# Moving the early key and value sums of an attention and feed-forward kernel from VectorE and ScalarE to GpSimd, with a new order of instructions

## The chip, the cores and the metric

The kernel runs on one core of a Trainium2 chip. The metric is the time of one execution on the device in microseconds (us), as the median of several runs. Engines are named as in the profile: PE is TensorE, PEld its weight loads, DVE is VectorE, ACT is ScalarE, POOL is GpSimd, SP is the engine whose queue issues most of the transfers (SPq). All five work through their own queue strictly in order, and wait for each other by semaphores.

## What is computed

The reference is an attention with pooled keys and values, and a gated feed-forward layer on its result:

```python
k_p = k.reshape(B, H, Sp, pool, D).mean(axis=3)      # B=8, H=8, S=576, D=64, pool=8: 72 keys
v_p = v.reshape(B, H, Sp, pool, D).mean(axis=3)
scores = scale * np.matmul(q, k_p.transpose(0, 1, 3, 2))
scores = scores - np.max(scores, axis=-1, keepdims=True)
attn = np.exp(scores)
attn = attn / (np.sum(attn, axis=-1, keepdims=True) + 1e-09)
return np.matmul(attn, v_p)
...
x = attn_out.transpose(0, 2, 1, 3).reshape(B * S, H * D)      # 4608 x 512
gate = 1.0 / (1.0 + np.exp(-(x @ w_gate)))                    # w_gate, w_val 512 x 1536, w_out 1536 x 512
val = x @ w_val
return (gate * val @ w_out)
```

The mean over 8 neighbours of the sequence is made as a sum of 8; the factor 1/8 goes into the scale of the keys and into the denominators of the softmax. Weights arrive as 8-byte floats and are converted on the chip (w, raw), then split into a high and a low part (parts, oparts), so that three fast matmuls stand for one exact one.

## The kernel before, in words

The 4608 rows are cut into nine blocks of 512 rows, numbered j from 0. Heads go in pairs p (four pairs, 128 partitions). A block of 512 rows does not end where a batch of 576 ends, so block 1 needs the keys and values of batches 0 and 1, block 2 those of batches 1 and 2.

The function `first_pass` computes the attention of blocks 0, 1 and 2 and the feed-forward layer of block 0, while the weights arrive. Afterwards the blocks go two by two through a form that saves matmuls (`hidden`, `second_sums`), while the attention of later blocks (`attention`) is fitted in between. The change touches `first_pass` alone.

For the steps of this text, these names matter. In `first_pass`, `keys(j, p)` sums eight neighbours of the raw keys (a DVE reduction of 128x576 to 128x72 into the array that the profile calls early; raw, raws and h are the rooms of raw inputs). `place_keys` writes the two halves, scaled, into one of five buffers kbd, by two ACT instructions. `scores` multiplies queries with kbd on PE (tile sc); `maximum` and `exps` follow on DVE and ACT (tile e or early). `v_sum` and `r_sum` sum the raw values: the first 64 pooled values of each head on 128 partitions (128x512 to 128x64), the last eight on 96 partitions. `v_hi` casts a value sum (vh, ACT), `v_lo` subtracts (vl, DVE), `r_hi`, `r_lo` and `v_put` do the same for the last eight (other, vres), and `product_av` multiplies on PE. For block 0 the value sums are made by PE (vp, vr), for blocks 1 and 2 by DVE. `conv` steps turn raw weights into parts (four steps alternate between ACT and DVE), `product_of` makes the products with the gate and value weights (tile chain), `gate` and `h_of` apply the sigmoid (y) and multiply, `accumulate` multiplies with the third weight (tile acc).

The helper `pool(out, raw, eng)` is a single reduction on VectorE, and for another engine three additions of halves, in place in the raw tile:

```python
n = POOL // 2
while n > 1:
    eng.tensor_tensor(out=raw[:, :, :n], in0=raw[:, :, :n], in1=raw[:, :, n:2 * n], op=ALU.add)
    n //= 2
eng.tensor_tensor(out=out[:, :, None], in0=raw[:, :, :1], in1=raw[:, :, 1:2], op=ALU.add)
```

Every instruction of the whole program is first recorded by a small layer (`Book`, `Taken`), as units, and then issued in the order of the table LATER, a list of unit numbers. This table alone sets where an instruction stands in the queue of its engine; waits follow from the data. A second table, UNREAD, says how many matmuls with an unread result PE does ahead of some products (in the profile: sc, chain, av or tr, from cst or from kbd alone). Since all instructions go through the recording layer, the profile gives them one line (L319), and they are told apart by their tiles.

Of the kernel before, what the change touches and what calls it, by code (L numbers as in the profile page):

```python
# [61 lines left out]
    "sc.0.1.1": 10, "sc.0.1.0": 1, "sc.0.0.1": 1, "sc.0.2.0": 5, "sc.0.3.1": 7, "sc.0.3.0": 2, "sc.1.0.0": 1,  # L62
    "rturn.0.1": 5, "av.0.3": 1, "mm.0.0": 1, "mm.0.1": 5, "mm.1.0": 2, "mm.1.1": 1, "mm.0.2": 1, "sc.1.1.0": 1,
# [268 lines left out]
def attention_then_ffn(ctx: ExitStack, tc: tile.TileContext, qT, kT, vm, vr, vn, sums8, wgv, wo, const, out, outT):  # L332
# [759 lines left out]
    def first_pass():  # L1092
# [79 lines left out]
        def keys(j, p):  # L1172
            k = raws["k", j, p] if j else got[f"k{p}"].rearrange("p (g t) -> p g t", t=POOL)
            nc.vector.reduce_sum(out=ks[j, p][:, :KEYS], in_=k, axis=AX.X)
# [87 lines left out]
        def v_sum(j, p):  # L1262
            pool(vs[j, p], raws["v", j, p], nc.vector)
# [199 lines left out]
```

## Time and profile before

| what | value |
|---|---|
| median of 3 runs | 934.22 us (932.6 to 936.99) |
| the profiled execution, its own time | 933.27 us |
| its span, first to last instruction | 931.5 us |
| granted clock of TensorE over the span | 0.999 |
| busy: PE, DVE, ACT, POOL | 918.0, 695.0, 572.4, 24.1 us |
| instructions: PE, DVE, ACT, POOL | 4375, 1062, 1044, 59 |

The profiled execution takes 1.8 us beside its span, and lies 0.95 us below the median. Rows of a group read: engine, operation, output tile and inputs, shapes, count, then busy time in us and the mean of one in ns, then idle time of the engine in front of them and what ended it. A window row gives the busy time of each engine in a stretch of the span, with the number of instructions in brackets, then the granted clock, the mean share of the DMA engines and their rate. A busy PE is not PE at its peak, since matmuls overlap and their ends are modelled.

### The profile page before, as it was taken

Reading aid. Unit: us, or ns where it says so; the run is one execution under the profiler, and the core shown is the slowest. Engines: PE = TensorE matmul, PEld = TensorE weight load, DVE = VectorE, ACT = ScalarE, POOL = GpSimd, SP = SyncE. Lnnn points to the kernel's source line nnn. Section 1 sums busy time; section 2 is a strip of 40 time slices with the busy share of each in tenths; the row PEclk is TensorE's granted clock in tenths of the full one; section 3 lists DMA queues with packets and bytes.
Section 4 is the critical chain, followed back from the end, with each engine's and each line's share of the span. In section 5 each row is a group of like instructions: output and inputs, shape, how many; then the busy total and the mean of one; then the engine's idle time right before and its main releaser. Section 6 shows DMA issues by size and latency. Waiting matters only on the chain.

```text
span 931.5 us, 12557 instructions
## 1 busy us (share of the span) xinstructions
PE 918.0 (99%) x4375; PEld 756.0 (81%) x4375; DVE 695.0 (75%) x1062; ACT 572.4 (61%) x1044; POOL 24.1 (3%) x59
## 2 busy tenths in 40 slices
PE   8999999999999999999999999999999999999998
PEld 7778788887888878888888888888888878888886
DVE  6998888899999997976789956464768573544763
ACT  7999998679989764665575636443554353234442
POOL 1000000011121000000000000000000000000000
PEclk9999999999999999999999999999999999999999
DMA  9999496778889757787667567545456675566266
GB/s 341 372 354 346 164 392 226 254 264 304 289 303 340 265 192 262 265 301 243 210 212 235 191 223 232 191 166 186 156 193 203 216 235 191 177 198 191 94 212 192
DMA packets 90367, 223.13 MB, mean 240 GB/s; under 512 B 9536, under 2 KB 28480, under 8 KB 88768
## 3 DMA queue, kind: packets, MB, share of 16 engines
q1 hardware_dynamic: 85184, 203.97, 64.9%
q0 software_dynamic: 5120, 18.35, 5.1%
q8 instruction: 35, 0.57, 0.2%
q14 instruction: 28, 0.23, 0.1%
HBM read 168.81 MB, written 53.48 MB: 239 GB/s over the span
## 4 chain that ended last, share of the span: by engine, by line
PE 92%; ACT 5%; DMA 2%; DVE 1%; issue 0%; POOL 0%; ACTq 0%; POOLq 0%
PE chain L319 54%; PE acc L319 27%; PE sc L319 4%; PE av L319 4%; PE tp L319 2%; ACT e L319 1%; DMA parts<-keptV0C 1%; DMA oparts<-keptS 1%; ACT w L319 1%; ACT L319 1%; DMA oparts<-keptO 0%; ACT raw L319 0%; ACT y L319 0%; PE vp L319 0%; ACT parts L319 0%
## 5 line engine op out<-in xcount | busy, mean ns | idle before, releaser
L319 PE MATMUL chain<-xo,parts 128*128 128x512 f32 x2316 | 558.6, 394 | 2.9 <-ACT y L319 1.4
L319 PEld LDWEIGHTS chain<-xo,parts 128*128 128x128 f32 x2316 | 427.2, 188 | 93.4 <-ACT y L319 2.1
L319 PE MATMUL acc<-hs,oparts 128*128 128x512 f32 (+1 forms) x1011 | 235.3, 390 | 0.8 <-DMA oparts<-keptO 0.5
L319 PEld LDWEIGHTS acc<-hs,oparts 128*128 128x128 f32 x1011 | 188.2, 188 | 41.6 <-issue 1.4
L319 DVE TENSOR_TENSOR hs<-h,hs 128x1024 fp32r<-128x1024 f32 x52 | 63.3, 1221 | 37.9 <-ACT hs L319 37.5
L319 ACT CAST hs<-h 128x1024 fp32r<-128x1024 f32 x52 | 54.6, 1053 | 52.6 <-PE acc L319 51.4
L319 DVE TENSOR_TENSOR y<-chain,sG 128x512 f32<-128x512 f32 x69 | 47.2, 686 | 45.6 <-PE chain L319 32.3
L319 DVE TENSOR_TENSOR y<-chain,sV 128x512 f32<-128x512 f32 x69 | 47.2, 686 | 37.3 <-PE chain L319 25.8
L319 ACT COPY sV<-chain 128x512 f32<-128x512 f32 x69 | 40.3, 586 | 52.4 <-PE chain L319 48.6
L319 ACT COPY sG<-chain 128x512 f32<-128x512 f32 x69 | 40.4, 586 | 48.3 <-PE chain L319 47.7
L319 ACT ACTIVATE gate<-y 128x512 f32<-128x512 f32 x69 | 43.2, 631 | 39.7 <-DVE y L319 35.2
L319 ACT CAST hs<-s 128x1024 fp32r<-128x1024 f32 x36 | 37.9, 1054 | 39.8 <-PE acc L319 24.2
L319 ACT ACT_TABLE_LOAD x47 | 60.3, 1283 | 1.4 <-DVE y L319 0.5
L319 DVE TENSOR_TENSOR hs<-s,hs 128x1024 fp32r<-128x1024 f32 x36 | 44.0, 1221 | 14.6 <-ACT hs L319 14.4
L319 DVE TENSOR_TENSOR h<-y,gate 128x512 f32<-128x512 f32 x69 | 47.4, 689 | 3.8 <-ACT gate L319 1.8
L319 PE MATMUL sc<-kbd,raw 128*128 128x144 f32 (+1 forms) x260 | 41.0, 295 | 1.0 <-ACT other L319 0.7
L319 PEld LDWEIGHTS sc<-kbd,raw 128*128 128x128 f32 (+1 forms) x260 | 33.5, 177 | 9.8 <-issue 2.8
L319 PE MATMUL acc<-oparts,hs 128*128 128x512 f32 x144 | 37.8, 399 | 0.1
L319 DVE TENSOR_REDUCE m<-sc 128x4 f32<-128x288 f32 x48 | 21.7, 452 | 14.3 <-PE sc L319 14.0
L319 PEld LDWEIGHTS acc<-oparts,hs 128*128 128x128 f32 x144 | 26.3, 188 | 5.5 <-ACT pr L319 0.3
L319 DVE TENSOR_TENSOR h<-h 128x256 f32<-128x256 f32 (+2 forms) x39 | 28.3, 728 | 0.7
L319 ACT ACTIVATE gate<-chain 128x512 f32<-128x512 f32 x23 | 13.8, 599 | 18.9 <-PE chain L319 18.5
(193 smaller groups left out, 1026.0 us busy)
## 6 DMA issues: line engine op xcount, KB each, us to landing
oparts<-keptS SPq DMA_DIRECT2D x48, 512.0 KB, 4.1
oparts<-keptO SPq DMA_DIRECT2D x72, 256.0 KB, 3.5
raw<-in_wgv SPq DMA_DIRECT2D x12, 1024.0 KB, 8.7
out<-o SPq DMA_DIRECT2D x35, 256.0 KB, 4.4
raw<-in_kT SPq DMA_DIRECT2D x28, 288.0 KB, 4.8
raw<-in_qT SPq DMA_DIRECT2D x29, 256.0 KB, 4.4
raw_o<-in_wo SPq DMA_DIRECT2D x12, 512.0 KB, 6.7
keptO<-oparts SPq DMA_DIRECT2D x12, 512.0 KB, 3.8
```

Of the source, the lines that this page charges most:

```text
L319: return self._book.take(lambda: f(*args, **named))
```

## The change

For blocks 1 and 2 the sums of keys (8), of values (8) and of the last values (4) go from one VectorE reduction each to three GpSimd additions each, and the 16 ScalarE instructions that place scaled keys become 16 GpSimd instructions. Block 0 stays as it was. The list of steps of the first pass (ORDER) is the same; the table UNREAD holds other numbers, and the table LATER is another one.

```diff
 UNREAD = {
-    "sc.0.1.1": 10, "sc.0.1.0": 1, "sc.0.0.1": 1, "sc.0.2.0": 5, "sc.0.3.1": 7, "sc.0.3.0": 2, "sc.1.0.0": 1,
-    "rturn.0.1": 5, "av.0.3": 1, "mm.0.0": 1, "mm.0.1": 5, "mm.1.0": 2, "mm.1.1": 1, "mm.0.2": 1, "sc.1.1.0": 1,
+    "sc.0.1.1": 9, "sc.0.1.0": 1, "sc.0.0.1": 4, "sc.0.0.0": 6, "sc.0.2.1": 3, "sc.0.2.0": 3, "sc.0.3.1": 4,
+    "rturn.0.0": 1, "turn.0.1": 2, "sc.0.3.0": 5, "sc.1.0.1": 3, "av.0.0": 1, "rturn.0.1": 2, "turn.0.3": 1,
+    "av.0.3": 1, "mm.0.0": 3, "mm.0.1": 1, "mm.1.1": 1,
 }
...
 LATER = """
-2 17 15 11 34 5 10 35 19 14 6 36 12 8 3 37 18 4 7 38 16 9 39 13 28 40 41 20 42 43 24 46 58 90 25 91 92 23 26 93 94 79
...
         def keys(j, p):
             k = raws["k", j, p] if j else got[f"k{p}"].rearrange("p (g t) -> p g t", t=POOL)
-            nc.vector.reduce_sum(out=ks[j, p][:, :KEYS], in_=k, axis=AX.X)
+            pool(ks[j, p][:, :KEYS], k, nc.gpsimd if j else nc.vector)
...
             for r, c in ((slice(0, D), slice(0, KEYS)), (slice(D, P), slice(KEYS, 2 * KEYS))):
-                nc.scalar.activation(t[r, c], ks[j, p][r, :KEYS], AF.Copy, scale=SCALE)
+                if j:
+                    nc.gpsimd.tensor_scalar(out=t[r, c], in0=ks[j, p][r, :KEYS], scalar1=SCALE, scalar2=None, op0=ALU.mult)
+                else:
+                    nc.scalar.activation(t[r, c], ks[j, p][r, :KEYS], AF.Copy, scale=SCALE)
...
         def v_sum(j, p):
-            pool(vs[j, p], raws["v", j, p], nc.vector)
+            pool(vs[j, p], raws["v", j, p], nc.gpsimd if j else nc.vector)
...
         def r_sum(j, g):
-            pool(vsr[j, g][:96], raws["r", j, g], nc.vector)
+            pool(vsr[j, g][:96], raws["r", j, g], nc.gpsimd if j else nc.vector)
```

What the new table and the new engine make of the queues is seen in the order of the instructions. First GpSimd, at the start of the program, before: the last zeroing of buffers (vh, vl), and behind it the transfers of the next stage (keptG4A and the like).

```order
L319 MEMSET kbd_90 128x144
L319 MEMSET vh_93 128x128
L319 MEMSET vl_102 128x128
L319 MEMSET vh_95 128x128
L319 MEMSET vl_99 128x128
L319 DMA keptG4A<-parts 128x1024
L319 DMA keptG4B<-parts 128x1024
```

The same place with the change (raw is a raw tile of values or of keys, early the array of the sums, kbd_92 a buffer of placed keys):

```order
L322 MEMSET vl_100 128x128
L322 MEMSET vl_101 128x128
L322 MEMSET vl_102 128x128
L322 ISA
L322 TENSOR_TENSOR raw<-raw 128x64x4
L322 TENSOR_TENSOR raw<-raw 128x64x2
L322 TENSOR_TENSOR early<-raw 128x64
L322 TENSOR_TENSOR raw<-raw 128x72x4
L322 TENSOR_TENSOR raw<-raw 128x72x2
L322 TENSOR_TENSOR early<-raw 128x72
L322 TENSOR_SCALAR kbd_92<-early 64x72
```

A value sum, a key sum and its placing come in between, and a new instruction ISA ahead of the first addition, which the built program calls a reload of the library of GpSimd. The transfers of the next stage stand behind all 76 new arithmetic instructions.

Second VectorE, in the first pass, where weights are converted, before (w and raw_o are weights on the way, parts and oparts their split form, sc the scores):

```order
L319 TENSOR_REDUCE early<-raw 128x72
L319 TENSOR_TENSOR parts<-w_259,parts 128x2x256
L319 TENSOR_SCALAR w_265<-w_265 128x1024
L319 TENSOR_TENSOR parts<-w_245,parts 128x2x256 x2
L319 SCALAR_TENSOR_TENSOR w_265<-w_265,raw_225 128x1024
L319 TENSOR_SCALAR w_o<-w_o 128x1024
L319 TENSOR_REDUCE early<-raw 128x72
L319 SCALAR_TENSOR_TENSOR w_o<-w_o,raw_o 128x1024
L319 TENSOR_REDUCE early<-raws 96x64
L319 TENSOR_REDUCE early<-sc 128x4
L319 TENSOR_REDUCE early<-raw 128x72
```

The same place with the change:

```order
L322 TENSOR_REDUCE early<-sc 128x4
L322 TENSOR_SCALAR w_259<-w_259 128x1024
L322 TENSOR_TENSOR parts<-w_245,parts 128x2x256
L322 TENSOR_TENSOR vl_102<-early,vh_97 64x64
L322 TENSOR_TENSOR parts<-w_245,parts 128x2x256
L322 SCALAR_TENSOR_TENSOR w_259<-w_259,raw_226 128x1024
L322 TENSOR_SCALAR w_o<-w_o 128x1024
L322 SCALAR_TENSOR_TENSOR w_o<-w_o,raw_o 128x1024
L322 TENSOR_TENSOR parts<-w_259,parts 128x2x256
L322 TENSOR_TENSOR h<-chain,y 128x512
```

Four reductions of raw tiles are gone from eleven rows, what is left is conversion of weights, and the first product of the feed-forward layer (h) has moved up into it.

Third ScalarE at the start, with the change: the exponentials of block 0 (e, early), and among them the cast vh_97 of the value sum that GpSimd makes first.

```order
L322 ACTIVATE e<-sc,early 128x72 x8
L322 ACTIVATE kbd_91<-early 64x72 x2
L322 ACTIVATE early<-sc,early 128x72 x4
L322 CAST vh_97<-early 64x64
L322 ACTIVATE w_235<-raw_221 128x1024
L322 ACTIVATE early<-sc,early 128x72 x5
L322 ACTIVATE raw_221<-raw_221,cst 128x1024
```

And the same place before:

```order
L319 ACTIVATE e<-sc,early 128x72 x5
L319 ACTIVATE early<-sc,early 128x72 x4
L319 CAST vh_97<-early 64x64
L319 ACTIVATE kbd_91<-early 64x72
L319 ACTIVATE w_235<-raw_221 128x1024
L319 ACTIVATE early<-sc,early 128x72 x2
L319 ACTIVATE raw_221<-raw_221,cst 128x1024
```

The cast keeps its place, ahead of the first conversion of weights (w_235); what it waits for is now made by GpSimd in place of VectorE.

307 rows, old and new, of the table LATER are left out of this document.

## The prediction

> **What bounds the kernel now.** I read the page first: it says which engine the whole span hangs on.
>
> ```profile
> span 931.5 us, 12557 instructions
> PE 92%; ACT 5%; DMA 2%; DVE 1%; issue 0%; POOL 0%; ACTq 0%; POOLq 0%
> ```
>
> The second line is the chain of waits that ended last. PE holds 92% of it, ScalarE 5% (about 47 us), VectorE 1%. So the change, which adds no useful PE work and removes none, can only gain where PE stands behind ScalarE or VectorE. Busy time by stage shows where that is:
>
> ```profile
> core 0: us, PE busy (x) PEld busy (x) DVE busy (x) ACT busy (x) POOL busy (x), PEclk, DMA share, GB/s
> 0.00:20.00 20.00, 16.29 (x107) 15.01 (x108) 12.07 (x25) 13.25 (x45) 2.48 (x19) 1.00 0.94 328
> 20.00:60.00 40.00, 37.69 (x200) 29.51 (x199) 38.69 (x69) 37.76 (x80) 0.00 (x0) 1.00 1.01 385
> 60.00:100.00 40.00, 39.90 (x199) 32.56 (x198) 36.95 (x62) 37.80 (x82) 0.00 (x0) 1.00 0.85 297
> 100.00:160.00 60.00, 58.88 (x296) 48.01 (x295) 48.31 (x77) 56.26 (x107) 0.00 (x0) 1.00 0.71 272
> 160.00:400.00 240.00, 238.62 (x1151) 195.15 (x1150) 222.48 (x371) 179.76 (x354) 21.60 (x40) 1.00 0.80 275
> 400.00:931.50 531.50, 526.62 (x2433) 435.73 (x2431) 336.50 (x461) 247.60 (x384) 0.00 (x0) 1.00 0.62 201
> ```
>
> From 20 to 160 us ScalarE is busy 131.8 of 140 us. VectorE is as full to 60 us (38.69 of 40) and then loosens, to 48.31 of 60. PE is idle only 2.31 + 0.10 + 1.12 = 3.5 us there, and from 160 us on 6.3 us, most of it at the very end. The granted clock is 1.00 throughout, so no clock is to be won. GpSimd does nothing from 20 to 160 us. The chain of waits, asked for 20 to 160 us alone, says who holds it there:
>
> ```profile
> by line: PE chain L319 35.7%; PE acc L319 18.8%; PE av L319 7.7%; PE sc L319 5.0%; ACT w L319 3.8%; ACT L319 3.7%; ACT e L319 3.4%; ACT raw L319 2.8%; ACT y L319 2.4%; ACT hs L319 1.3%; issue 1.3%; ACT early L319 1.1%; ACT parts L319 1.1%;
> ```
>
> The ScalarE names add to 19.6% of 140 us, 27.4 us; no VectorE name is among the thirteen largest. So in this stage it is ScalarE that PE waits for now and then, and VectorE hardly ever.
>
> **What leaves ScalarE.** Sixteen placements of scaled keys go.
>
> ```profile
> L319 ACT ACTIVATE kbd<-early 64x72 f32<-64x72 f32 x24 | 6.3, 263 | 2.5 <-DVE early L319 2.3
> ```
>
> Sixteen of these 24 at 263 ns are 4.2 us, fourteen of them inside 20 to 160 us. Upper bound of the gain: ScalarE's queue is the bound all along, and the whole 4.2 us reaches PE. Lower bound: the gain counts only while ScalarE holds the chain, so fourteen times 0.263 us, 3.7 us, times 27.4 / 131.8, which is 0.8 us. I take 2.5 us, the middle, because between 20 and 60 us both queues are so full that ScalarE's lead would show, and after 60 us PE has little idle time left to give.
>
> **What leaves VectorE.** Twenty reductions, by these rows for 5 to 110 us:
>
> ```profile
> L319 DVE TENSOR_REDUCE early<-raw 128x72 f32<-128x576 f32 x8 | 5.9, 742 | 0.0
> L319 DVE TENSOR_REDUCE early<-raws 128x64 f32<-128x512 f32 x4 | 2.7, 678 | 0.0
> L319 DVE TENSOR_REDUCE early<-raws 96x64 f32<-96x512 f32 x4 | 2.6, 672 | 0.0
> L319 DVE TENSOR_REDUCE early<-raw 128x64 f32<-128x512 f32 x3 | 2.0, 675 | 0.0
> L319 DVE TENSOR_REDUCE early<-early 128x64 f32<-128x512 f32 x1 | 0.7, 667 | 0.0
> ```
>
> 5.9 + 2.7 + 2.6 + 2.0 + 0.7 = 13.9 us. I put this at nothing: with VectorE shorter, ScalarE, which was as full, is late next. If that cover fails the gain is larger (first rival).
>
> **What comes to GpSimd.** Sixty additions and sixteen placements. No row shows arithmetic there; the nearest are its zeroing of a kbd buffer and VectorE's own two-input work at the same sizes:
>
> ```profile
> L319 POOL MEMSET kbd<- 128x144 f32 x5 | 1.0, 221 | 0.3 <-POOLq L1454 0.3
> L319 DVE TENSOR_TENSOR parts<-h,parts 128x256 fp32r<-128x256 f32 x9 | 3.7, 420 | 0.0
> L319 DVE TENSOR_TENSOR r<-rest,r 128x128 fp32r<-128x128 f32 x18 | 5.1, 283 | 0.5 <-ACT r L319 0.5
> L319 DVE TENSOR_TENSOR vl<-vs,vh 64x64 fp32r<-64x64 f32 x40 | 8.7, 217 | 4.7 <-ACT vh L319 4.0
> ```
>
> At VectorE's pace a sum is 0.42 + 0.28 + 0.22 = 0.92 us, twenty are 18.4 us, and sixteen placements at 0.22 us are 3.5 us: 22 us at least. At three times that pace it would be 59 us, still inside the 100 us or so over which the inputs arrive and are used, so the engine itself is no bound. The Trainium skill (GPSIMD Engine Reference, section Performance versus the Vector engine) gives 4497 ns against VectorE's 2293 ns for an addition of 2048 elements; by that factor 1.96 the additions would be 36 us and the whole, as an estimate, 40 us.
>
> Where the new queue waits: each placement waits until PE has read the old keys, and the sums behind it stand still meanwhile. The placement of kbd_89, for one, waits for the first scores from a kbd and raws, with later sums behind it. In the chain of waits they are this piece:
>
> ```profile
> 43.62 0.84 PE sc L319 x6
> ```
>
> The sums behind belong to scores and products much later than that, so I put it at nothing. The weight transfers of the next stage stand behind all this on the same queue, but their first was issued after an idle time of 162.7 us:
>
> ```profile
> L319 POOL DMA_DIRECT2D keptG4A<-parts x1 | 0.7, 671 | 162.7 <-DVE parts L319 162.7
> ```
>
> So 22 to 59 us of new work ahead of them cost nothing.
>
> **What moves on SP and PE.** The first load of values goes from seventh to fourth place in SP's queue. At the 328 GB/s of the first window its 256 KB hold the loads behind it back by 0.8 us; between 0 and 0.8 us, I take 0.3 us, since only half of block 0's first loads stand behind it. The unread matmuls go from 44 to 51. What they cost is seen in the rows for 20 to 60 us:
>
> ```profile
> L319 PE MATMUL chain<-cst 128*128 128x128 f32 x20 | 3.3, 286 | 0.9 <-DVE xo L319 0.9
> L319 PE MATMUL tr<-cst 128*128 128x128 f32 x10 | 1.3, 282 | 0.0
> L319 PE MATMUL sc<-cst 128*128 128x128 f32 x4 | 0.8, 273 | 0.0
> L319 PE MATMUL av<-cst 128*128 128x128 f32 x2 | 0.4, 275 | 0.0
> ```
>
> Each counts as two instructions, 0.33 us by the first row, so seven more are 2.3 us at most. They stand where PE waits anyway, so I take nothing, and nothing up to 2.3 us for the range. The new table moves everything else as well, up to the last stage; the 6.3 us of PE idle time after 160 us is what it could win, and by the same measure lose. I take 0, and 2 us to either side.
>
> **The sum.** 933.27 - 2.5 + 0.3 = 931.1 us for the profiled execution; it lay 0.95 us below the median of the runs, so the median to expect is 932.0 us. Its own range is 928 to 938.5 us: 934.2 - 4.2 - 2 one way; 934.2 - 0.8 + 0.8 + 2.3 + 2 the other.
>
> **Rival one: VectorE's relief counts too.** From 20 to 60 us it is the fuller of the two (38.69 us), and nine of the twenty reductions start between these two, its timeline says:
>
> ```profile
> 37.74 0.74 DVE L319 TENSOR_REDUCE early<-raw 128x72 f32<-128x576 f32 x1
> ...
> 58.48 0.75 DVE L319 TENSOR_REDUCE early<-raw 128x72 f32<-128x576 f32 x1
> ```
>
> Then the two queues shrink together, and what PE gives up is its waiting: the 3.5 us of idle time and the 3.3 + 1.3 + 0.8 + 0.4 = 5.8 us of unread matmuls of 20 to 60 us, 9.3 us at most. With 8 us of it gone the median is 926.2 us. For it speaks the order, in which the first h stands among the conversions and not after them; against it that the chain has no VectorE name of weight, and that UNREAD has grown.
>
> **Rival two: GpSimd's additions hold VectorE up.** Work on tiles in memory that VectorE does with two inputs, or at twice its pace, is the bulk of its load from 5 to 110 us:
>
> ```profile
> L319 DVE TENSOR_TENSOR parts<-w,parts 128x512 fp32r<-128x512 f32 x18 | 12.2, 684 | 1.7 <-ACT parts L319 1.6
> L319 DVE SCALAR_TENSOR_TENSOR w<-w,raw 128x1024 uint32<-128x1024 uint32 x9 | 11.0, 1219 | 0.7 <-ACT raw L319 0.6
> L319 DVE TENSOR_SCALAR w<-w 128x1024 f32<-128x1024 f32 x9 | 6.2, 684 | 0.6 <-ACT w L319 0.6
> ```
>
> If every GpSimd instruction kept such work waiting for its whole time, VectorE would get back 22 us for the 13.9 us it loses, 8 us net, of which the 1.31 + 3.05 = 4.4 us that it is idle from 20 to 100 us swallow half. The 3.7 us left are more than ScalarE's 2.5 us; add 0.3 us of SP, and the median is 935.7 us; with half as many meetings VectorE breaks even and the forecast stands. Before, the two engines never worked side by side in this stage, so no row speaks for or against it. The Trainium skill (SBUF — State Buffer, section Who interferes with whom) says just this: a VectorE instruction with two inputs in SBUF, and a GpSimd instruction that reads SBUF, exclude each other, the second waits for the first to end. By that rule alone, with the 40 us estimated above all spent in VectorE's way, 40 - 13.9 - 4.4, 21.7 us, would come on top of the forecast: 954 us, as an estimate; I don't expect so many meetings, since reductions and work on PSUM are free of it.
>
> **Rival three, slower: the first sum comes too late.** ScalarE's cast of a value sum stands in front of its first conversion of weights, and nothing passes it. These rows are from the timelines of POOL, DVE, ACT and PE:
>
> ```profile
> 2.81 0.20 POOL L319 MEMSET vl<- 128x128 f32 x1
> 11.43 0.68 DVE L319 TENSOR_REDUCE early<-raw 128x64 f32<-128x512 f32 x1
> 14.13 0.26 ACT L319 CAST vh<-early 64x64 fp32r<-64x64 f32 x1
> 17.01 0.74 DVE L319 TENSOR_REDUCE early<-raw 128x72 f32<-128x576 f32 x1
> 21.75 0.91 PE L319 MATMUL sc<-kbd,raw 128*64 128x144 f32 x6
> ```
>
> GpSimd is free at 3.0 us and ScalarE asks at 14.1 us; PE's first scores of block 1 ask for the first placed keys at 21.75 us. In between stand the new ISA instruction, a reload of code that no row prices, and 0.92 us of additions, twice that before the keys. Each microsecond that the first sum ends after 14.1 us is lost on ScalarE, and through it on PE. The rival decides from 14.1 + 4.7 + 2.2 = 21 us on, when reload and sum take 18 us; at 24 us the loss is 9.9 us, against 2.2 us gained, and the median is 941.9 us. The Trainium skill (GPSIMD Engine Reference, section Instruction dispatch) puts the load of code ahead of a first call at about 6 us; by that, as an estimate, the sum is there at about 10 us and this rival falls.
>
> **How the numbers follow.** About 0.5%, 4.7 us, is what a measurement of this kernel can tell from no change. Forecast (932.0 us) 0.42; rival one (926.2 us) 0.25; rival two (935.7 us) 0.14; rival three (941.9 us and more) 0.19. Faster than 929.5 us are rival one and the lower end of the forecast, together 0.31. Slower than 938.9 us are rival three but for its mild end, 0.17, and the bad end of rival two, 0.06: 0.23. The rest, 0.46, is no change that can be told. The range 924 to 942 us leaves out the far half of rival three and a little of rival one.
>
> **What would show it.** Right: kbd and the sums leave ACT and DVE, GpSimd is busy 22 to 60 us more, ScalarE's share of the chain from 20 to 160 us is a little smaller, and PE reaches the same matmuls of the next stage 2 to 3 us earlier. Rival one: PE's idle time and unread matmuls in 20 to 60 us shrink by more than 5 us. Rival two: the mean of parts, 684 ns, or of w, 1219 ns, grows in the first 100 us. Rival three: a wait of ScalarE's vh or PE's sc for POOL before 30 us. The prediction is wrong at its root if the difference arises after 160 us, from the table alone.

## The result, and the profile after

With the change the kernel takes 929.18 us (median of eight runs, 928.23 to 932.44), and 934.72 us without it in the same series: a ratio of 0.9947, 95% interval 0.9931 to 0.9963. By this ratio it is 5 us less, within 3.5 and 6.4 (the two medians lie 5.5 us apart). The forecast was 932.0 us, 2.2 us less; the measured time lies inside its range of 924 to 942 us, on the edge between "no change" and "faster". The profiled execution took 929.36 us. Its page, span and busy times:

```profile
span 927.5 us, 12645 instructions
PE 916.7 (99%) x4389; PEld 758.9 (82%) x4389; DVE 690.1 (74%) x1042; ACT 568.0 (61%) x1028; POOL 76.2 (8%) x135
PE 83%; ACT 5%; DVE 4%; DMA 3%; issue 3%; POOL 1%; SPq 0%; POOLq 0%; ACTq 0%; DVEq 0%
```

GpSimd has 52.1 us more (76.2 against 24.1), within the 22 to 59 us foreseen. ScalarE has 4.4 us less, as it should. VectorE has lost 13.9 us of reductions but is only 4.9 us shorter: something gave most of it back. (Not all 9 us of that is owed to GpSimd's reading: in the run e7 below, where GpSimd only fills, VectorE is 10.5 us shorter than before, at 684.5 us, so the reading takes 5.6 us.) Its rows up to 112 us, to be laid beside the 684 and 1219 ns of before, with three of the additions and the placements behind them:

```profile
L322 DVE TENSOR_TENSOR parts<-w,parts 128x512 fp32r<-128x512 f32 x18 | 15.0, 846 | 0.6 <-ACT parts L322 0.5
L322 DVE SCALAR_TENSOR_TENSOR w<-w,raw 128x1024 uint32<-128x1024 uint32 x9 | 12.3, 1369 | 0.4
L322 DVE TENSOR_TENSOR oparts<-w_o,oparts 128x1024 fp32r<-128x1024 f32 x3 | 4.6, 1523 | 0.0
L322 POOL TENSOR_SCALAR kbd<-early 64x72 f32<-64x72 f32 x16 | 10.3, 641 | 26.9 <-PE sc L322 26.0
L322 POOL TENSOR_TENSOR raw<-raw 128x288 f32<-128x288 f32 x8 | 6.9, 860 | 11.4 <-DMA raw<-in_kT 11.4
L322 POOL TENSOR_TENSOR raw<-raw 128x144 f32<-128x144 f32 x8 | 5.6, 701 | 0.5
L322 POOL TENSOR_TENSOR early<-raw 128x72 f32<-128x72 f32 x8 | 3.4, 421 | 0.6
```

The work of VectorE with two inputs in memory has grown: 18 × 0.162 + 9 × 0.150 + 3 × 0.31, with oparts at 1213 ns before, is 5.2 us in these three rows. That is the mechanism of rival two, here with the forecast's outcome. Rival three stayed away: GpSimd waited for its data, and before 30 us nobody waited for a sum or for placed keys. GpSimd's timeline, and ScalarE's and PE's waits for it in the first 160 us:

```profile
6.17 1.20 POOL L322 TENSOR_TENSOR raw<-raw 128x256 f32<-128x256 f32 x2 [3.12 <-DMA raw<-in_vm]
7.45 0.30 POOL L322 TENSOR_TENSOR early<-raw 128x64 f32<-128x64 f32 x1
...
ACT vh L322 <- POOL early L322: 1.0, 1, 1.0
...
PE sc L322 <- POOL kbd L322: 1.0, 1, 1.0
```

The first sum is there at 7.75 us, and ScalarE's cast of before stood at 14.13 us. ScalarE's one wait for GpSimd ends at 89.70 us, for a later value sum. PE's one wait ends at 1.01 us, at its very first matmul, for the zeroing of a kbd buffer, and the kernel before has the same 1.0 us there: PE never waited for a sum or for placed keys. Between the last zeroing and the first addition lie 3.1 us, which is the most that the reload can have cost there. The Trainium skill (GPSIMD Engine Reference, section Instruction dispatch) gives about 6 us for it; the trace has no room for that much, unless part of it ran beside the zeroing, which it doesn't show.

The windows of the four stretches up to 160 us, for the number of PE's instructions:

```profile
0.00:20.00 20.00, 17.83 (x120) 17.14 (x121) 10.61 (x21) 12.10 (x42) 7.51 (x28) 1.00 0.93 344
20.00:60.00 40.00, 38.50 (x206) 30.79 (x205) 38.48 (x64) 37.32 (x74) 25.28 (x36) 1.00 0.99 363
60.00:100.00 40.00, 39.32 (x191) 31.74 (x190) 32.20 (x49) 36.46 (x75) 20.03 (x30) 1.00 0.83 305
100.00:160.00 60.00, 59.79 (x305) 49.70 (x304) 51.06 (x82) 56.32 (x107) 1.72 (x2) 1.00 0.75 287
```

PE has issued 822 matmuls by 160 us, against 802 before; 14 of the 20 are the seven additional unread ones. The six others say little: e3 below has the same first pass as the kernel before and counts 795. A better mark is the end of the first pass. Its last result is copied out by 176.35 us, against 177.61 us before, 1.3 us earlier; its last store is issued at 176.67 us, against 179.98 us, 3.3 us earlier. The two tables put different work around these two instructions, so neither is the exact share of the first pass in the 4.0 us by which the two profiled spans differ. The experiments ask for it.

### The profile page after: what moved, and what is told of

The parts are those of the page before. It is cut to its first block, busy times and chain, and to the rows that moved or that the text cites. A ratio compares the mean times of both kernels' runs of the same rounds, so it can differ in the third digit from the quotient of the medians.

```text
span 927.5 us, 12645 instructions
## 1 busy us (share of the span) xinstructions
PE 916.7 (99%) x4389; PEld 758.9 (82%) x4389; DVE 690.1 (74%) x1042; ACT 568.0 (61%) x1028; POOL 76.2 (8%) x135
## 4 chain that ended last, share of the span: by engine, by line
PE 83%; ACT 5%; DVE 4%; DMA 3%; issue 3%; POOL 1%; SPq 0%; POOLq 0%; ACTq 0%; DVEq 0%
PE chain L322 47%; PE acc L322 27%; PE sc L322 4%; PE av L322 3%; PE tp L322 2%; ACT e L322 1%; DMA keptV0C<-parts 1%; DMA parts<-keptG2A 1%; DVE w L322 1%; DMA raw<-in_vr 1%; DMA oparts<-keptS 1%; ACT w L322 1%; DMA raw<-in_kT 1%; ACT L322 1%; ACT parts L322 0%
## 5 line engine op out<-in xcount | busy, mean ns | idle before, releaser
L322 DVE TENSOR_TENSOR hs<-s,hs 128x1024 fp32r<-128x1024 f32 x36 | 43.8, 1219 | 13.8 <-ACT hs L322 13.8
L322 DVE TENSOR_REDUCE m<-sc 128x4 f32<-128x288 f32 x48 | 21.6, 450 | 11.2 <-PE sc L322 11.0
L322 ACT CAST ph<-tp 128x512 fp32r<-128x512 f32 x28 | 16.5, 588 | 17.4 <-PE tp L322 17.3
```

What stands on the lines that cost most here:

```text
L322: return self._book.take(lambda: f(*args, **named))
```

## The experiments

Two things were changed at once: who does the work, and the order. The tables are lists of steps, so each order can be carried over to the other choice of engines: a reduction stands where the first of its three additions stood, and three additions where their reduction stood. All runs are compared with the kernel before in the same series; a microsecond figure is the ratio times 934.7. Intervals are about 1.5 us to either side, so differences of two such runs are known to about 2 us.

| run | order, engines | median, us | ratio (95%) | us against before | last store of the first pass, us |
|---|---|---|---|---|---|
| the change | new, GpSimd | 929.18 | 0.9947 (0.9931 to 0.9963) | -5.0 | 176.67 |
| e1 | new, old engines | 933.03 | 0.9989 (0.9974 to 1.0004) | -1.0 | 180.00 |
| e2 | old, GpSimd | 938.46 | 1.0049 (1.0032 to 1.0067) | +4.6 | 183.72 |
| e11 | old, placements alone on GpSimd | 935.93 | 1.0013 (0.9997 to 1.0030) | +1.2 | 179.82 |
| e10 | old, GpSimd fills | 935.30 | 1.0004 (0.9991 to 1.0018) | +0.4 | 179.80 |
| e6 | new, placements alone on GpSimd | 930.42 | 0.9953 (0.9940 to 0.9965) | -4.4 | 178.29 |
| e5 | new, sums alone on GpSimd | 931.94 | 0.9970 (0.9955 to 0.9984) | -2.8 | 178.00 |
| e7 | new, GpSimd fills | 925.22 | 0.9901 (0.9884 to 0.9918) | -9.3 | 171.72 |
| e8 | new, additions twice | 942.16 | 1.0077 (1.0062 to 1.0091) | +7.2 | 190.06 |
| e9 | new, placements and casts on GpSimd | 930.42 | 0.9947 (0.9929 to 0.9965) | -5.0 | 177.01 |
| e3 | old first pass, new behind it | 931.94 | 0.9975 (0.9960 to 0.9990) | -2.3 | 181.10 |
| e4 | new first pass, old behind it | 933.15 | 0.9986 (0.9972 to 1.0001) | -1.3 | 176.74 |
| e12 | new to 400 us, old behind it | 935.94 | 1.0007 (0.9995 to 1.0020) | +0.7 | 176.63 |

The last column is read from the profiled execution of each run, in the timeline of SP: when the fourth store of the result was issued, the last one of the first pass (179.98 us before). It shows where an edit of the first pass bears, free of what the later stages add, but only between runs with the same order of the first pass: before, e2, e3, e10 and e11 have the old one, the others the new. Two executions with the same first pass lie up to 1.1 us apart in it (before and e3), the three of the change, e4 and e12 only 0.1 us. Four profiled executions lie 2 to 3.5 us off the median of their runs: those of e3 (934.86 us), e4 (929.70 us), e5 (929.83 us) and e9 (933.55 us).

### One half at a time: e1, e2

The first run has the new order and the old engines:

```diff
-            pool(ks[j, p][:, :KEYS], k, nc.gpsimd if j else nc.vector)
+            pool(ks[j, p][:, :KEYS], k, nc.vector)
...
-            pool(vs[j, p], raws["v", j, p], nc.gpsimd if j else nc.vector)
+            pool(vs[j, p], raws["v", j, p], nc.vector)
...
-            pool(vsr[j, g][:96], raws["r", j, g], nc.gpsimd if j else nc.vector)
+            pool(vsr[j, g][:96], raws["r", j, g], nc.vector)
...
-                if j:
+                if False:
                     nc.gpsimd.tensor_scalar(out=t[r, c], in0=ks[j, p][r, :KEYS], scalar1=SCALE, scalar2=None, op0=ALU.mult)
```

> The new tables with the old engines: VectorE reduces and ScalarE places, each sum at the place of its first addition. Theory (about half of the 5 us comes from the engines, half from the table behind the first pass): the later 2 us stay and the first pass loses its gain, or more, since the table was made for other engines: 932 to 935 us. Rival, the table alone does it: 929 to 930 us. Rival, the engines alone do it: 934.7 us or slower.

The second has the changed code with the two old tables, LATER and UNREAD.

> The old tables with the new engines: GpSimd adds and places at the places where VectorE reduced and ScalarE placed. Theory: the first pass gains its 2 us, nothing comes behind it: 932 to 933.5 us. Rival, the engines alone do it: 929.5 us. Rival, the table alone does it: 934.7 us or slower. If VectorE's relief is eaten by its meetings with GpSimd, the mean of parts is about 0.8 us here too, against 0.684 us before.

Measured: -1.0 us and +4.6 us, the second clear of zero. e1 fell where the theory had it. e2 missed it by 5 us; it lies where one rival had it (the table alone does it, 934.7 us or slower), but e1 speaks against that rival: the order alone brings little, and the engines alone cost. In the old order GpSimd holds VectorE up more than in the new one: VectorE is busy 693.6 us in e2 and 684.0 us with fills (e10), 9.6 us apart, against 5.6 us between the change and e7. VectorE's rows of e2 up to 112 us:

```profile
L314 DVE TENSOR_TENSOR parts<-w,parts 128x512 fp32r<-128x512 f32 x17 | 14.8, 883 | 2.1 <-ACT parts L314 2.0
L314 DVE SCALAR_TENSOR_TENSOR w<-w,raw 128x1024 uint32<-128x1024 uint32 x9 | 12.0, 1337 | 0.5 <-ACT raw L314 0.3
L314 DVE TENSOR_SCALAR w<-w 128x1024 f32<-128x1024 f32 x9 | 7.6, 839 | 2.6 <-ACT w L314 2.6
```

### The reliefs without the new order: e11, e10

The forecast's main term was ScalarE's relief, by itself. It can be had alone, in the old order, with one edit of the kernel before:

```diff
-                nc.scalar.activation(t[r, c], ks[j, p][r, :KEYS], AF.Copy, scale=SCALE)
+                if j:
+                    nc.gpsimd.tensor_scalar(out=t[r, c], in0=ks[j, p][r, :KEYS], scalar1=SCALE, scalar2=None, op0=ALU.mult)
+                else:
+                    nc.scalar.activation(t[r, c], ks[j, p][r, :KEYS], AF.Copy, scale=SCALE)
```

> The kernel before with one thing changed: the sixteen placements of blocks 1 and 2 are GpSimd's, at their old places in the old tables; all sums stay on VectorE. By the forecast's step ScalarE's relief reaches PE by itself: 2.5 us less, between 0.8 and 4.2 us, so 930.5 to 933.9 us. Rival, formed from the fills in the old order: a relief reaches PE only where the order uses it, so no difference, 934 to 936 us.

And both reliefs without the additions' reading, as e2 with fills:

```diff
-    eng.tensor_tensor(out=raw[:, :, :n], in0=raw[:, :, :n], in1=raw[:, :, n:2 * n], op=ALU.add)
+    eng.memset(raw[:, :, :n], 0.0)
...
-    eng.tensor_tensor(out=out[:, :, None], in0=raw[:, :, :1], in1=raw[:, :, 1:2], op=ALU.add)
+    eng.memset(out[:, :, None], 0.0)
```

> The old tables with the new engines (938.5 us), but with GpSimd filling with zeros instead of adding; the sums of blocks 1 and 2 are left out. If the 4.6 us that the move costs in the old order come from the meetings, they go, and with VectorE's and ScalarE's relief kept it is 929 to 931 us. If they come from the order (a queue of GpSimd in which sums and placements stand in each other's way), it stays at 936 us or more.

Measured: +1.2 us (-0.3 to +2.8) and +0.4 us. The relief alone brings nothing that shows in the old order, not even with VectorE's 13.9 us on top; the first pass ends 0.2 us earlier in both. PE's three longest waits are the same to a tenth: first those from 20 to 160 us before the change, then in e11.

```profile
PE chain L319 <- ACT y L319: 1.4, 2, 1.1
PE chain L319 <- DVE xo L319: 0.9, 1, 0.9
PE sc L319 <- ACT other L319: 0.7, 1, 0.7
```

```profile
PE chain L313 <- ACT y L313: 1.4, 2, 1.2
PE chain L313 <- DVE xo L313: 0.9, 1, 0.9
PE sc L313 <- ACT other L313: 0.6, 1, 0.6
```

ScalarE itself now waits longer for PE, up to 160 us before and in e11: with y, the sigmoid of a product, and with parts, a conversion that waits there for PE's products:

```profile
ACT y L319 <- PE chain L319: 1.6, 2, 1.3
ACT parts L319 <- PE chain L319: 0.3, 1, 0.3
```

```profile
ACT y L313 <- PE chain L313: 2.3, 2, 1.9
ACT parts L313 <- PE chain L313: 0.8, 1, 0.8
```

The longest of PE's waits shows how the relief is lost. Before, ScalarE places keys four times between 38.73 and 46.52 us, waits 0.27 us for PE and starts the conversion parts at 47.05 us; from there it works without a gap to the y at 58.06 us for which PE waits.

```profile
45.56 0.26 ACT L319 ACTIVATE kbd<-early 64x72 f32<-64x72 f32 x1
46.52 0.26 ACT L319 ACTIVATE kbd<-early 64x72 f32<-64x72 f32 x1
47.05 0.62 ACT L319 CAST parts<-w 128x512 fp32r<-128x512 f32 x1 [0.27 <-PE chain L319]
58.06 1.09 ACT L319 ACTIVATE y<-chain 128x512 f32<-128x512 f32 x2
```

In e11 the four placements are gone, but ScalarE waits 0.48 us for VectorE at 44.67 us and 0.80 us for PE, and the same conversion starts at 47.18 us, the same y at 58.20 us. So less work for ScalarE becomes idle time of ScalarE at the next thing that it needs from another engine; PE's wait hangs on ScalarE's queue behind that point, and no placement stood there. Of the 4.6 us of e2, 4.2 us go when GpSimd stops reading. That is the most that the meetings can have cost there: fills also end sooner than additions, and waits for GpSimd's sums, 0.9 us of PE and 0.5 us of ScalarE in e2, are gone in e10 as well. By its expectation e10 should have fallen to 929 to 931 us; it did not, since the reliefs bring nothing in this order.

### The reliefs in the new order, one by one: e6, e5, e9

e6 leaves only the placements on GpSimd (the first three edits of e1); e5 leaves only the sums there (the last edit of e1).

> The changed kernel with the twenty sums back on VectorE, each at the place of its first addition; only the placements are on GpSimd. The forecast's step (ScalarE's relief is what counts): 929.5 to 930.5 us. Rival one (VectorE's relief counts too): 932 to 933 us. Meetings nearly gone: mean of parts 0.69 to 0.72 us.

> The changed kernel with the sixteen placements back on ScalarE, at their places in the same order; only the sums are on GpSimd. The forecast's step (ScalarE's relief is what counts): the 4 us between the new order with old engines (933 us) and with new ones (929.2 us) are lost, about 933 us. Rival one (VectorE's relief counts too): most of the 4 us stay, 930 us. The meetings stay: mean of parts about 0.85 us by either.

Measured: -4.4 us and -2.8 us, against -1.0 us with neither (e1) and -5.0 us with both. e6 fell where the forecast's step had it; e5 lies between the two values foreseen. The placements bring 3.4 us on top of e1. The sums bring 1.8 us without the placements and 0.6 us on top of them, neither clear of nothing. The end of the first pass shares it out more evenly: 180.00 us in e1, 178.29 us with the placements, 176.67 us with the sums as well, so 1.7 us for the placements and 1.6 us for the sums. These are single executions, and the two accounts agree within the 2 us to which the medians are known. In e6 VectorE works undisturbed:

```profile
L314 DVE TENSOR_TENSOR parts<-w,parts 128x512 fp32r<-128x512 f32 x18 | 12.1, 683 | 0.0
L314 DVE SCALAR_TENSOR_TENSOR w<-w,raw 128x1024 uint32<-128x1024 uint32 x9 | 11.0, 1220 | 0.3
```

If ScalarE's relief counts in this order, more of it should count more. e9 is e6 with GpSimd also casting value sums:

```diff
-                    nc.scalar.copy(vh[i][r, r], vs[j, p][r])
+                    nc.gpsimd.tensor_copy(vh[i][r, r], vs[j, p][r])
...
-            nc.scalar.copy(vrc[j, g], vsr[j, g][:96])
+            nc.gpsimd.tensor_copy(vrc[j, g], vsr[j, g][:96])
```

> The run in which GpSimd only places keys (930.4 us), and beside the placements GpSimd now casts the value sums of blocks 1 and 2 in ScalarE's stead: sixteen casts of 64x64 at 240 ns and four of 96x64 at 250 ns, 4.8 us less for ScalarE. If what counts is ScalarE's relief, at the rate that the sixteen placements showed (3.4 us for 4.2 us), 926.5 to 927.5 us. Rival: VectorE's queue, full from 20 to 60 us and still with all its sums, is now the later one, and nothing more comes: 930 to 931 us.

Measured: -5.0 us, 0.6 us from e6 and not to be told from it. ScalarE has 2.8 us less (565.6 against 568.4 us busy), and it brings nothing that shows. By the medians the rate of 0.8 us per microsecond fell, and the rival's outcome came. (The first pass ends at 177.01 us, 1.3 us before e6's; from one execution each, that leaves a smaller rate open.) Its reason fits the window of 20 to 60 us, in which VectorE, with all its sums, is busy 39.21 of 40 us; but e1 and e6 have the same 39.21 us there, so this cause is argued, not shown:

```profile
20.00:60.00 40.00, 35.92 (x192) 28.40 (x191) 39.21 (x72) 35.62 (x69) 5.40 (x9) 1.00 1.01 363
```

### The meetings by themselves: e7, e8

e7 is the change with the fills of e10.

> The changed kernel with GpSimd filling the same places with zeros instead of adding, so that it writes but doesn't read; the sums of blocks 1 and 2 are left out. If only reading keeps VectorE waiting, parts falls back to about 0.69 us and VectorE keeps all its 13.9 us. Then, if VectorE's relief counts, the time falls by 2 to 4 us below that of the change, to 925 to 927.5 us; if ScalarE is late next, as the forecast has it, it stays at 929 us. If writing locks as well, parts stays above 0.8 us.

e8 adds to each addition a second one that nobody reads:

```diff
+    with book.unit():
         eng.tensor_tensor(out=raw[:, :, :n], in0=raw[:, :, :n], in1=raw[:, :, n:2 * n], op=ALU.add)
+        eng.tensor_tensor(out=raw[:, :, n:2 * n], in0=raw[:, :, n:2 * n], in1=raw[:, :, n:2 * n], op=ALU.add)
...
```

> The changed kernel with every GpSimd addition followed by a second one of the same size, of the dead upper half to itself: the computation stays whole, GpSimd's additions double to some 85 us. If each meeting holds VectorE up, parts goes to about 1.0 us and VectorE gets back another 9 us; if that counts, 932 to 935 us. If VectorE's time is covered by ScalarE and GpSimd's sums are early enough anyway, 929 to 930 us.

Measured: -9.3 us and +7.2 us. In e7 VectorE's durations are back, and its busy time falls by 11.2 us (684.5 against 695.7 in e1), where that of the change falls by 5.6 (to 690.1). VectorE up to 112 us, then its last two stretches of the first pass:

```profile
L316 DVE TENSOR_TENSOR parts<-w,parts 128x512 fp32r<-128x512 f32 x21 | 14.1, 689 | 1.9 <-ACT parts L316 1.7
L316 DVE SCALAR_TENSOR_TENSOR w<-w,raw 128x1024 uint32<-128x1024 uint32 x11 | 13.5, 1226 | 0.4
...
20.00:60.00 40.00, 39.38 (x216) 32.00 (x215) 36.63 (x64) 38.78 (x75) 10.35 (x35) 1.00 1.01 366
60.00:100.00 40.00, 40.00 (x201) 33.13 (x200) 31.60 (x54) 38.13 (x77) 9.47 (x31) 1.00 0.82 317
```

PE issues 417 matmuls from 20 to 100 us, 20 more than with the change, and the first pass ends 5.0 us earlier (171.72 against 176.67 us). So VectorE's relief would be worth about 4 us more, if the sums didn't have to read. (The sums are also ready earlier in e7; but of ScalarE and PE only ScalarE waited for a sum in the changed kernel, 1.0 us, so that is at most a part.) e8 came out 7 us above the upper of its two foreseen ranges, and parts takes 897 ns there, not the 1.0 us foreseen. It can't be put down to meetings alone: GpSimd is busy 37.3 of the 40 us from 20 to 60 us, and its sums come late. PE stood still more than with the change (busy 33.50 and 36.56 of 40 us in the two windows from 20 to 100 us), and its granted clock was 0.97 in both, against 1.00 with the change. These are waits of e8 up to 160 us (1.0 us of the last row is the zeroing at the start):

```profile
ACT vh L316 <- POOL early L316: 5.9, 1, 5.9
ACT other L316 <- POOL early L316: 3.9, 1, 3.9
...
PE sc L316 <- POOL kbd L316: 4.0, 4, 2.5
```

That is rival three's mechanism, from a full queue and not from a reload.

### What the order behind the first pass is worth: e3, e4, e12

These have no edit of the code: the table is put together from the two, the first part from one, the rest in the order of the other. e3 is the kernel before, with the new order behind the last store of the first pass; e4 and e12 are the changed kernel, with the old order behind that store, or from 400 us on.

> The kernel before up to the last instruction of the first pass, and behind it the order of the new table. Theory: 2 us less, 932.5 to 933 us. Rival, all of the gain arises in the first pass: 934.7 us, no difference. Rival, all of it comes from the table behind the first pass: 929.5 to 930 us.

> The changed kernel up to the last instruction of the first pass, and behind it the order of the old table. Theory: about 2 of the 5 us are lost, 931 to 932 us. Rival, all of the gain arises in the first pass: 929.2 us as with the change. Rival, all of it comes from behind: 934.7 us.

> The changed kernel up to 400 us, and behind it the order of the old table. Cut behind the first pass it lost 3 to 4 us against the change (933.2 us). If the later gain lies between 176 and 400 us, it is as fast as the change, 929 to 930 us; if it lies behind 400 us, 932 to 933.5 us; if it is spread, in between, 930.5 to 932 us.

Measured: -2.3, -1.3 and +0.7 us. All three lie somewhat outside what was foreseen (e3 half a microsecond below, e4 1 us above, e12 about 2 us above). The new order behind the first pass is worth 2.3 us by e3, and 3.7 us by the distance from e4 to the change. A cut should cost rather than gain, since what one order sends ahead can come late in the other; e12 shows such a case, in PE's waits from 390 us on (and its granted clock fell to 0.98 between 400 and 500 us), and so doesn't say where the later gain lies:

```profile
PE chain L316 <- DMA parts<-keptG2A: 3.4, 1, 3.4
PE chain L316 <- DMA parts<-keptV0C: 0.6, 1, 0.6
```

Which of the later stages gains stays open, and single profiles are a poor guide to it: from the last store of the first pass to the end, the change takes 750.8 us and e4, with the old order there, 750.9 us; the kernel before takes 751.5 us and e3, with the new order there, 752.0 us. That shows none of the 2 us, but e3's profiled execution lies 2.9 us above the median of its runs and e4's 3.4 us below. What differs is PE's waits for transfers after 160 us. With the old order behind the first pass they add to 1.6 us before, 3.5 in e2, 3.0 in e11, 1.2 in e10 and 0.4 in e4. With the new order they add to 0.2 to 0.7 us in seven runs, the change among them (0.4), and to 2.1 us in e3. So they are 1.3 us less on average with the new order, and the two that stand out, e4 and e3, are the two whose time stands out the same way. That makes them the likely place of the gain, not a shown one: no run has changed them alone.

## Why the prediction was right, and where not

- **ScalarE's relief, -2.5 us: the size was right, the reason was not.** In the new order the placements bring 3.4 us by the medians and 1.7 us by the end of the first pass (e1 to e6), within the bounds of 0.8 to 4.2 us. But the step had it that "ScalarE's lead would show" by itself, and e11 shows that it doesn't: nothing in the old order. The 19.6% of ScalarE in the chain of waits doesn't tell which of ScalarE's work counts: what was taken away ahead of its next wait for another engine, as ahead of 47 us, changed nothing.
- **VectorE's relief at nothing: near enough, but wrong in its cover.** The sums bring 0.6 us by the medians, which is not clear of nothing, and 1.6 us by the end of the first pass. What kept it small was not that "ScalarE is late next": without the meetings it would be worth about 4 us more (e7). Rival one had the mechanism (the two queues shrink together), rival two had what hinders it. That the two nearly cancel is luck; the forecast's sum had neither.
- **Rival two's price.** It reckoned with 22 us of held work; three rows show 5.2 us in the new order. "With half as many meetings VectorE breaks even and the forecast stands" is near to what happened: a quarter as many, and VectorE 4.9 us shorter. In time the meetings cost at most 4.2 us in the old order (e2 against e10) and at most 4.3 us in the new one (the change against e7). So the rule of the Trainium skill (SBUF — State Buffer, section Who interferes with whom) that was weighed there holds in this case, at a price well below the 21.7 us estimated from it, since only 5.6 us (new order) and 9.6 us (old) of GpSimd's 52 us of new work stood in VectorE's way.
- **GpSimd's own time at nothing: right in the main** at 52.1 us: ScalarE waited for it once, 1.0 us, and its sums of raws now hold 2.5% of the chain of waits from 20 to 160 us; e8 shows that it stops being free when the queue is full from 20 to 100 us.
- **The table behind 160 us, 0 with 2 us to either side: mis-sized.** This is the step that, by the medians, makes 2.2 us into 5: it is worth 2.3 us (e3, within 0.9 and 3.7). "Wrong at its root" was to be said if all the difference arose there; by the medians about half of it does, and by the two profiled spans between 0.7 and 2.7 of 4.0 us lie behind the first pass, depending on the mark taken for its end.
- **The unread matmuls at nothing, the 0.3 us of SP:** nothing measured contradicts them, and no run tells them apart. (The first load of values came from the ninth place in SP's queue, not the seventh: two rows of the timeline hold two loads each.)
- **The range:** 924 to 942 us holds the prices of all four outcomes weighed (926.2, 932.0, 935.7 and 941.9 us), so that the time lies in it says little about the steps.

The 5 us, put together from the medians of the runs: -2.3 for the order behind the first pass (e3), +1.3 for the new first-pass order with old engines (e1 less e3), -3.4 for the placements (e6 less e1), -0.6 for the sums. Only the first and third are clear of nothing.

## What to carry to other kernels

A share of the chain of waits tells whose answer is late, not that any work taken from that engine will make it earlier: here relief ahead of the engine's next wait was lost in that wait, and counted only in a new order. So try the edit in the old order and the new order without the edit before believing in either. In these runs work handed to GpSimd was not free for VectorE while it read memory with two inputs: compare the mean of VectorE's unchanged instructions before and after. A new table changes the stages that the edit doesn't touch, and here that was worth about 2 us of 5 by the medians. A single profile can be an odd execution: see where it lies among its runs before reading a wait of 1 us from it.

## What the runs showed of the hardware

Where additions on GpSimd ran beside two-input work on VectorE, both took longer; beside fills VectorE didn't, and beside placements, with one input, hardly. VectorE's one-input TENSOR_SCALAR on w took longer too, 839 against 684 ns in e2, and its reductions of scores did not (451 against 452 ns). These rows give the shortest, median and longest in ns: the additions and VectorE's parts in the changed kernel,

```profile
L322 POOL TENSOR_TENSOR early<-raw x11: 298/319/814, 7.4 to 75.2; 128x72 f32<-128x72 f32 x8, 128x64 f32<-128x64 f32 x3
L322 DVE TENSOR_TENSOR parts<-w,parts x18: 675/752/1494, 22.3 to 106.7; 128x512 fp32r<-128x512 f32 x18
```

and the placements and parts in e6, where GpSimd does nothing else:

```profile
L314 POOL TENSOR_SCALAR kbd<-early x16: 381/390/2272, 20.7 to 106.7; 64x72 f32<-64x72 f32 x16
L314 DVE TENSOR_TENSOR parts<-w,parts x18: 672/681/732, 21.6 to 108.3; 128x512 fp32r<-128x512 f32 x18
```

One placement took 1.9 us more than the shortest, while parts never took more than 732 ns (693 before). In e7, where GpSimd only writes but for the placements, parts stayed at 739 ns at most, and in e10 at 694. The page of the Trainium skill named above says that a two-input instruction of VectorE contends with a GpSimd instruction that reads, and not with one that only writes; the fills agree. It would have the placements hold VectorE up as well when they come first; sixteen of them show no case of more than 0.05 us.
